# A diffusion block on one core: the half chunk that two heads share in row and column tiles, and LN2's scale and shift of batch 0 on two engines

## Chip, core, metric

One core of a Trainium2 chip runs the whole block. The metric is device time in microseconds (us), median over executions.

## The reference, cut to what matters

```python
B, N, D = (2, 256, 1152); F = 4 * D; H = 2; Dh = D // H          # Dh = 576 = 4.5 * 128
mod = (_silu(c) @ w_mod).reshape(B, 6, 1, D)
shift_a, scale_a, gate_a, shift_m, scale_m, gate_m = [mod[:, i] for i in range(6)]
h = _layernorm(x, axis=-1) * (1 + scale_a) + shift_a
qkv = (h @ wqkv).reshape(B, N, 3, H, Dh)
attn = _softmax(jnp.einsum('bqhd,bkhd->bhqk', q, k) * Dh ** (-0.5), axis=-1)
a = jnp.einsum('bhqk,bkhd->bqhd', attn, v).reshape(B, N, D) @ wo
x = x + gate_a * a
h2 = _layernorm(x, axis=-1) * (1 + scale_m) + shift_m            # "LN2"
m = _gelu(h2 @ w_fc1) @ w_fc2                                    # "FC1", "FC2"
return x + gate_m * m
```

The features are worked on in nine chunks of 128. A head has 576 of them, so chunk 4 (`HC` in the code) holds the last 64 features of head 0 and the first 64 of head 1. That is the shared chunk.

## The kernel before, the parts that matter

The masks for the shared chunk are zero-padded copies of k and v, cleared by four memsets on GpSimd at the start:

```python
    kT4m = act.tile([P, H, T], BF16, name="kT4m")
    v4m = act.tile([P, NT, H, P], BF16, name="v4m")
    nc.gpsimd.memset(kT4m[HP:P, 0, :], 0.0)
    nc.gpsimd.memset(kT4m[0:HP, 1, :], 0.0)
    nc.gpsimd.memset(v4m[:, :, 0, HP:P], 0.0)
    nc.gpsimd.memset(v4m[:, :, 1, 0:HP], 0.0)
```

Evictions from PSUM alternate between VectorE and ScalarE by a counter (`evac`). A score tile is five matmuls of 128 rows, and one score tile goes ahead of each of the first eight V groups:

```python
        for i, cc in enumerate(chunks):              # score_tile(b, h, qt); five chunks a head
            if cc == HC:
                k_ap = kT4m[:, h, b * N:(b + 1) * N]
            else:
                k_ap = kT[:, cc, b * N:(b + 1) * N]
            nc.tensor.matmul(
                ps_s[:], qT[:, cc, q0:q0 + P], k_ap,
                start=(i == 0), stop=(i == len(chunks) - 1),
            )
        # ... [cut: maximum, Exp with row sum, scaling]
    for i, (pnl, t) in enumerate(v_order):
        fin = score_tile(*score_order[i]) if i < len(score_order) else None
        v_group(pnl, t)
```

In the values stage the shared chunk takes four matmuls a batch (two heads, two key tiles, `v4m` as the stationary operand), every other chunk two. Then come the Wo groups, with LN2's statistics, normalisation and a DMA transpose per row tile of 128 tokens (row tiles 0 and 1 are batch 0), and LN2's scale and shift of the transposed chunks, all of them on VectorE:

```python
    def ln2_modulate(b, k):
        h = hT[:, k, b * N:(b + 1) * N]
        return nc.vector.tensor_scalar(
            h, h, scale_m[:, k, b:b + 1], shift_m[:, k, b:b + 1], op0=ALU.mult, op1=ALU.add,
        )
    # ... [cut]
    BETWEEN = {2: (0, 1), 3: (5,)}      # chunks done inside the normalisation of row tiles 2 and 3
    # ... [cut]
    for o, (t, i) in enumerate(order):
        if o == len(order) - 1:
            ln2_modulate(0, 2)
            ln2_modulate(0, 3)
        wo_group(t, i, i < NPD - 1)
        if o:
            ln2_stats(*order[o - 1])
    ln2_modulate(0, 4)
    ln2_stats(*order[-1])
    for k in range(6, KD):
        ln2_modulate(0, k)
```

FC1 starts with batch 0, six output chunks side by side, chunk by chunk: six matmuls per LN2 chunk.

The end of the kernel: the product of the last FC2 group with the gate, the addition of x1, and a 32 KB transfer of the output. For all other output groups the addition is on GpSimd.

## Time and profile before

| | before |
|---|---|
| time, median of 3 | 248.32 us (248.09 to 248.48) |
| span of the profiled execution | 246.4 us |
| TensorE (PE) busy | 238.0 us, 97% |
| VectorE, ScalarE, GpSimd busy | 67.0, 62.5, 28.0 us |
| first score to first value matmul (starts) | 52.27 to 76.83 us |
| FC1 to FC2, first matmuls | 98.74 to 172.49 us |

The share of busy time says only that TensorE bounds the kernel. Where it loses time is read from the chain of waits, which is followed back from the last instruction. Its columns are start, duration (us), and engine, tile and line of the kernel.

```profile
76.99 4.37 PE pa L545 x40
81.36 4.40 PE pacc L588 x27
85.76 0.02 issue
85.78 0.57 DVE tmp L593
...
104.61 0.27 DVE hT L559
104.87 0.04 issue
104.92 20.03 PE pacc L637 x181
...
172.66 70.30 PE pacc L691 x468
```

From 85.8 to 104.9 us VectorE (DVE) leads the chain, since it makes LN2 for FC1 (`L637`). The timeline of TensorE alone shows what that costs: start, duration, line, tiles, shape, number, and in brackets the idle time before and what ended it.

```profile
98.26 0.65 PE L588 MATMUL pacc<-w_o,big 128*128 128x384 bf16 x3
98.74 1.47 PE L637 MATMUL pacc<-hT,w_f 128*128 128x256 bf16 x12
100.66 1.47 PE L637 MATMUL pacc<-hT,w_f 128*128 128x256 bf16 x12 [0.44 <-DVE hT L559]
102.69 1.75 PE L637 MATMUL pacc<-hT,w_f 128*128 128x256 bf16 x12 [0.56 <-DVE hT L559]
104.92 3.33 PE L637 MATMUL pacc<-hT,w_f 128*128 128x256 bf16 x29 [0.48 <-DVE hT L559]
```

Thirty-six matmuls at 0.109 us each would take 3.9 us; the 37th starts 6.2 us after the first. The bracketed waits sum to only 1.5 us, because the ends of matmuls are modelled: measure such a hole from start to start.

The scores, in the same view. Four whole chunks and the masked one follow each other at the common pace of 0.109 us, and the V group starts one such step after them:

```profile
54.27 0.60 PE L468 MATMUL ps_s<-big 128*128 128x256 bf16 x4
54.71 0.27 PE L468 MATMUL ps_s<-kT4m,big 128*128 128x256 bf16 x1
54.82 1.63 PE L492 MATMUL pacc<-w_v,hT 128*128 128x384 bf16 x9
```

And the last 4 us. The first line counts all packets; the second gives a queue's packets, megabytes and share of time; the last two are transfers with their size and the time from issue to landing.

```profile
DMA packets 288, 0.10 MB, mean 25 GB/s; under 512 B 160, under 2 KB 288, under 8 KB 288
q1 hardware_dynamic: 288, 0.10, 9.3%
...
out_dram<-o_sb SPq DMA_DIRECT2D x1, 64.0 KB, 1.5
out_dram<-o_sb SPq DMA_DIRECT2D x1, 32.0 KB, 1.5
```

### The profile page before, as it was taken

How to read it: one execution, taken by the hardware profiler on the slowest of the kernel's cores; microseconds unless marked ns; L12 is line 12 of the kernel's file. 1: busy time of each engine (PE TensorE's matmuls, PEld its weight loads, DVE VectorE, ACT ScalarE, POOL GpSimd, SP SyncE). 2: the span in 40 equal slices, each digit the busy share in tenths (PEclk: the TensorE clock that was granted, in tenths of full speed). 3: DMA queues.
4: the chain of work that ended last, by engine and by line, in shares of the span. 5: the costliest groups of instructions: out<-in, count | busy, mean ns of one | idle time of the engine just before them, and what ended most of it. 6: DMA issues, size and time to landing. Idle time of an engine off the chain costs nothing.

```text
span 246.4 us, 3980 instructions
## 1 busy us (share of the span) xinstructions
PE 238.0 (97%) x1700; PEld 143.9 (58%) x1711; DVE 67.0 (27%) x184; ACT 62.5 (25%) x124; POOL 28.0 (11%) x43
## 2 busy tenths in 40 slices
PE   6999999999999999799999999999999999999994
PEld 2585444456657666588854444444666666666674
DVE  2852461335444598940000000000011000000001
ACT  6631341243423322361432233222000000000000
POOL 4000000031000234100000003100011212111111
PEclk9999999999999999999999999999999999999999
DMA  6999999999996998239999999990000000000100
GB/s 225 326 335 362 368 331 388 391 390 395 282 376 157 401 392 112 48 66 395 392 391 345 327 292 269 326 343 26 0 16 19 16 17 16 19 17 16 34 17 16
DMA packets 47373, 53.29 MB, mean 216 GB/s; under 512 B 8427, under 2 KB 34171, under 8 KB 47355
## 3 DMA queue, kind: packets, MB, share of 16 engines
q1 hardware_dynamic: 39840, 50.14, 60.9%
q10 hardware_dynamic: 6939, 1.71, 4.8%
q0 software_dynamic: 576, 1.19, 1.4%
q8 instruction: 13, 0.21, 0.4%
q14 instruction: 5, 0.04, 0.1%
HBM read 50.14 MB, written 1.19 MB: 208 GB/s over the span
## 4 chain that ended last, share of the span: by engine, by line
PE 88%; DVE 7%; DMA 2%; ACT 1%; issue 1%; DVEq 0%; ACTq 0%
PE pacc L691 29%; PE pacc L637 27%; PE pacc L492 7%; PE pacc L440 7%; PE pk L269 4%; PE pk L302 2%; PE pwarm L162 2%; PE pacc L588 2%; PE pa L545 2%; PE ps_s L468 2%; DVE stats L602 2%; PE pn L385 1%; DVE tmp L593 1%; DMA hT<-xn 1%; PE pg L418 1%; DMA c_sb<-in_c_dram 1%
## 5 line engine op out<-in xcount | busy, mean ns | idle before, releaser
L637 PE MATMUL pacc<-hT,w_f 128*128 128x256 bf16 (+1 forms) x427 | 70.9, 325 | 1.9 <-DVE hT L559 1.5
L691 PE MATMUL pacc<-w_f,gT 128*128 128x384 bf16 (+2 forms) x468 | 70.5, 314 | 0.0
L637 PEld LDWEIGHTS <-w_f 128*128 128x128 bf16 x432 | 42.1, 98 | 30.1 <-issue 2.5
L691 PEld LDWEIGHTS <-gT 128*128 128x128 bf16 x468 | 44.4, 98 | 26.2
L697 DVE TENSOR_TENSOR tmp<-pacc,gate 128x384 f32<-128x384 f32 (+2 forms) x13 | 6.8, 527 | 88.2 <-PE pacc L691 88.2
L669 ACT ACTIVATE gT<-pacc 128x512 bf16<-128x512 f32 x24 | 14.3, 597 | 32.2 <-PE pacc L637 32.2
L699 POOL TENSOR_TENSOR o_sb<-tmp,x 128x384 bf16<-128x384 f32 (+1 forms) x12 | 11.7, 971 | 73.8 <-DVE tmp L697 73.8
L492 PE MATMUL pacc<-w_v,hT 128*128 128x384 bf16 x108 | 19.2, 326 | 0.0
L440 PE MATMUL pacc<-hT,w_q 128*128 128x512 bf16 x79 | 17.7, 379 | 0.1
L588 PE MATMUL pacc<-w_o,big 128*128 128x384 bf16 x108 | 17.7, 326 | 0.0
L429 POOL DMA_DIRECT2D gates_dram<-nat x8 | 4.3, 543 | 93.5 <-DVE nat L426 93.5
L588 PEld LDWEIGHTS <-big 128*128 128x128 bf16 x108 | 10.6, 98 | 6.9
L492 PEld LDWEIGHTS <-hT 128*128 128x128 bf16 x108 | 10.4, 98 | 6.3 <-issue 0.5
L269 PE MATMUL pk<-big,w_k 128*128 128x256 bf16 (+2 forms) x88 | 13.3, 292 | 0.5 <-ACT big L256 0.4
L440 PEld LDWEIGHTS <-w_q 128*128 128x128 bf16 x81 | 7.8, 98 | 9.7 <-DMA w_q<-in_wqkv_dram 0.3
L426 DVE CAST nat<-pg 2x288 bf16<-2x288 f32 x4 | 1.8, 450 | 37.0 <-PE pg L418 36.9
L594 POOL TENSOR_TENSOR x<-tmp,x_sb 128x384 f32<-128x384 f32 x8 | 7.3, 914 | 35.9 <-DVE tmp L593 35.9
L269 PEld LDWEIGHTS <-w_k 128*128 128x128 bf16 x90 | 7.5, 97 | 3.4 <-DMA w_k<-in_wqkv_dram 0.3
L658 ACT ACTIVATE gT<-pacc 128x512 bf16<-128x512 f32 x12 | 6.6, 596 | 10.8 <-PE pacc L637 10.8
L162 PE MATMUL pwarm<-zeros 128*128 128x512 bf16 x18 | 7.3, 571 | 1.2 <-DVE eps_t L93 1.2
L593 DVE TENSOR_TENSOR tmp<-pacc,gate 128x384 f32<-128x384 f32 x12 | 6.6, 547 | 2.4 <-PE pacc L588 2.4
L288 DVE TENSOR_SCALAR big<-pacc 128x512 bf16<-128x512 f32 x5 | 3.5, 692 | 13.7 <-PE pacc L440 13.7
(94 smaller groups left out, 154.2 us busy)
## 6 DMA issues: line engine op xcount, KB each, us to landing
w_f<-in_w_fc_dram SPq DMA_DIRECT2D x14, 864.0 KB, 8.9
w_f<-in_w_fc_dram SPq DMA_DIRECT2D x2, 2592.0 KB, 12.4
w_f<-in_w_fc_dram SPq DMA_DIRECT2D x2, 1728.0 KB, 10.2
w_shift_a<-in_w_mod_dram SPq DMA_DIRECT2D x3, 864.0 KB, 11.5
w_q<-in_wqkv_dram SPq DMA_DIRECT2D x3, 864.0 KB, 12.1
w_gate_a<-in_w_mod_dram SPq DMA_DIRECT2D x3, 864.0 KB, 10.1
w_v<-in_wqkv_dram SPq DMA_DIRECT2D x3, 864.0 KB, 13.4
w_shift_m<-in_w_mod_dram SPq DMA_DIRECT2D x3, 864.0 KB, 15.3
```

The costliest lines, as they stand in the source:

```text
L162: nc.tensor.matmul(dst[:], zeros[:, 0:P], zeros[:], start=True, stop=True)
L269: nc.tensor.matmul(pk[m][:, c0:c1], w_k[:, k, m * P:(m + 1) * P], hT0[:, k, c0:c1], start=(k == 0 and c0 == 0), stop=(k == KD - 1), skip_g ...
L440: nc.tensor.matmul(pacc[:], w_q[:, k, m * P:(m + 1) * P], hT[:, k, :], start=(k == 0), stop=(k == KD - 1),)
L492: nc.tensor.matmul(pacc[:], hT[:, k, t * P:(t + 1) * P], w_v[:, k, pnl * PW:(pnl + 1) * PW], start=(k == 0), stop=(k == KD - 1),)
L588: nc.tensor.matmul(pacc[:], aT[:, k, t * P:(t + 1) * P], w_o[:, k, c0:c1], start=(k == 0), stop=(k == KD - 1),)
L593: nc.vector.tensor_tensor(tmp[:], pacc[:], gate_a[:, b, c0:c1], op=ALU.mult)
L594: (nc.gpsimd if pool_add else nc.vector).tensor_tensor(x1[:, t, c0:c1], tmp[:], x_sb[:, t, c0:c1], op=ALU.add)
L637: nc.tensor.matmul(dst, w_f1[m // KD][:, k, ml * P:(ml + 1) * P], hT[:, k, c0:c1], start=start, stop=(k == KD - 1), **kw,)
L669: nc.scalar.activation(gT[:, m, :], pacc[:], ACT.Gelu_apprx_tanh)
L691: nc.tensor.matmul(pacc[:], gT[:, kk, t * P:(t + 1) * P], w_f2[j][:, r, c0 - n * PW:c0 - n * PW + cw], start=(kk == 0), stop=(kk == KF - 1),)
L697: nc.vector.tensor_tensor(tmp[:], pacc[:], gate_m[:, b, c0:c0 + cw], op=ALU.mult)
L699: (nc.vector if last else nc.gpsimd).tensor_tensor(o_sb[:], tmp[:], x1[:, t, c0:c0 + cw], op=ALU.add)
```

## The change

The intent has two parts. First, the zero padding wastes half of each shared-chunk matmul; with 64 rows (scores) or 64 columns (values) each, the two heads' halves can run in two parts of the array at once. Second, LN2's scale and shift of batch 0 no longer all queue on VectorE: ScalarE takes chunks 2, 3, 5 and 7.

```diff
-    kT4m = act.tile([P, H, T], BF16, name="kT4m")
-    v4m = act.tile([P, NT, H, P], BF16, name="v4m")
-    nc.gpsimd.memset(...)                        # [cut: four of them]
     def k_evac(m):
-        if m == HC:
-            evac(kT4m[0:HP, 0, :], pk[m][0:HP, :])
-            evac(kT4m[HP:P, 1, :], pk[m][HP:P, :])
-        else:
-            evac(kT[:, m, :], pk[m][:])
+        evac(kT[:, m, :], pk[m][:])
+    def half(h):
+        return slice(h * HP, (h + 1) * HP)
+    def score_pair(b, qt):                       # replaces score_tile(b, h, qt)
+        ps = [acc_tile([P, N], "ps_s") for _ in range(H)]
+        for h in range(H):
+            whole = range(0, HC) if h == 0 else range(HC + 1, KD)
+            for cc in whole:
+                nc.tensor.matmul(ps[h][:], qT[:, cc, q0:q0 + P], kT[:, cc, b * N:(b + 1) * N],
+                                 start=(cc == whole[0]), stop=False)
+        for h in range(H):
+            nc.tensor.matmul(ps[h][:], qT[half(h), HC, q0:q0 + P], kT[half(h), HC, b * N:(b + 1) * N],
+                             start=False, stop=True)
         # ... [cut: maximum, Exp, scaling, now for two tiles]
-        c4 = HC * P - pnl * PW                   # [cut: the copies into v4m]
+    SCORES_AT = {0: (0, 0), 1: (0, 1), 3: (1, 0), 4: (1, 1)}
+    TRANSPOSES_AT = {3: 0, 7: 1}
         # ... [cut: the old order of the scores, and the loop that uses these two]
                     if cc == HC:                 # values, inside the loop over key tiles
+                        for h in range(H):
+                            nc.tensor.matmul(dst[half(h), :, :], vt[:, half(h)], attnT(b, h, kc),
+                                             start=(kc == 0), stop=(kc == TPB - 1))
         # ... [cut: the whole chunks, as before; the lines that this replaces]
-    def ln2_modulate(b, k):
+    def ln2_modulate(b, k, eng="d"):
+        if eng == "a":
+            return nc.scalar.activation(h, h, ACT.Identity, bias=shift_m[:, k, b:b + 1],
+                                        scale=scale_m[:, k, b:b + 1])
-    BETWEEN = {2: (0, 1), 3: (5,)}
+    BETWEEN = {2: ((0, "d"), (1, "d"), (2, "a"), (3, "a")), 3: ((8, "d"),)}
-        if o == len(order) - 1:
-            ln2_modulate(0, 2)
-            ln2_modulate(0, 3)
+        last = o == len(order) - 1
+        if last:
+            ln2_modulate(0, 4)
         wo_group(t, i, i < NPD - 1)
         if o:
             ln2_stats(*order[o - 1])
-    ln2_modulate(0, 4)
+        if last:
+            ln2_modulate(0, 5, "a")
+            ln2_modulate(0, 7, "a")
+            ln2_modulate(0, 6)
     ln2_stats(*order[-1])
-    for k in range(6, KD):
-        ln2_modulate(0, k)
```

More of the change, by code (lines that the diff above doesn't have):

```diff
@@ L144 @@
     HP = Dh - HC * P
-    kT4m = act.tile([P, H, T], BF16, name="kT4m")
-    v4m = act.tile([P, NT, H, P], BF16, name="v4m")
-    nc.gpsimd.memset(kT4m[HP:P, 0, :], 0.0)
-    nc.gpsimd.memset(kT4m[0:HP, 1, :], 0.0)
-    nc.gpsimd.memset(v4m[:, :, 0, HP:P], 0.0)
-    nc.gpsimd.memset(v4m[:, :, 1, 0:HP], 0.0)
     early = small.tile([P, 2], FP32, name="early", tag="early", bufs=1)
@@ L446 @@
             gate_a = gate_natural(0, w_gate_a)
-    def head_chunks(h):
-        return list(range(HC + 1)) if h == 0 else list(range(HC, KD))
+    def half(h):
+        return slice(h * HP, (h + 1) * HP)
     n_s = B * H * TPB
@@ L456 @@
     attnT_all = soft[:, 3 * n_s * N:4 * n_s * N].rearrange("p (i n) -> p i n", n=2 * N)
-    attn_tiles = {}
-    def score_tile(b, h, qt):
-        chunks = head_chunks(h)
+    def score_pair(b, qt):
         q0 = b * N + qt * P
-        ps_s = acc_tile([P, N], "ps_s")
-        for i, cc in enumerate(chunks):
-            if cc == HC:
-                k_ap = kT4m[:, h, b * N:(b + 1) * N]
-            else:
-                k_ap = kT[:, cc, b * N:(b + 1) * N]
+        ps = [acc_tile([P, N], "ps_s") for _ in range(H)]
+        for h in range(H):
+            whole = range(0, HC) if h == 0 else range(HC + 1, KD)
+            for cc in whole:
+                nc.tensor.matmul(
+                    ps[h][:], qT[:, cc, q0:q0 + P], kT[:, cc, b * N:(b + 1) * N],
+                    start=(cc == whole[0]), stop=False,
+                )
+        for h in range(H):
@@ L468, in score_tile @@
             nc.tensor.matmul(
-                ps_s[:], qT[:, cc, q0:q0 + P], k_ap,
-                start=(i == 0), stop=(i == len(chunks) - 1),
-            )
-        negmax = small.tile([P, 1], FP32, name="negmax", tag="negmax")
-        nc.vector.reduce_max(negmax[:], ps_s[:], axis=AX.X, negate=True)
-        si = (b * H + h) * TPB + qt
-        e_sb = e_all[:, si, :]
-        rowsum = small.tile([P, 1], FP32, name="rowsum", tag="rowsum")
-        nc.scalar.activation(e_sb, ps_s[:], ACT.Exp, bias=negmax[:], scale=1.0, accum_out=rowsum[:])
@@ L478, in score_tile @@
-        attn = attn_all[:, si, :]
-        attn_tiles[(b, h, qt)] = attn
+                ps[h][:], qT[half(h), HC, q0:q0 + P], kT[half(h), HC, b * N:(b + 1) * N],
+                start=False, stop=True,
+            )
+        parts = []
+        for h in range(H):
+            negmax = small.tile([P, 1], FP32, name="negmax", tag="negmax")
+            nc.vector.reduce_max(negmax[:], ps[h][:], axis=AX.X, negate=True)
+            si = (b * H + h) * TPB + qt
+            rowsum = small.tile([P, 1], FP32, name="rowsum", tag="rowsum")
+            nc.scalar.activation(
+                e_all[:, si, :], ps[h][:], ACT.Exp, bias=negmax[:], scale=1.0, accum_out=rowsum[:]
+            )
+            parts.append((si, rowsum))
@@ L481, in finish @@
         def finish():
-            rs = small.tile([P, 1], FP32, name="rs", tag="rs")
-            nc.vector.reciprocal(rs[:], rowsum[:])
-            nc.vector.tensor_scalar_mul(attn, e_sb, rs[:])
+            for si, rowsum in parts:
+                rs = small.tile([P, 1], FP32, name="rs", tag="rs")
+                nc.vector.reciprocal(rs[:], rowsum[:])
+                nc.vector.tensor_scalar_mul(attn_all[:, si, :], e_all[:, si, :], rs[:])
         return finish
@@ L496, in v_group @@
         evac(v_sb[:, t, pnl * PW:(pnl + 1) * PW], pacc[:])
-        c4 = HC * P - pnl * PW
-        if 0 <= c4 and c4 + P <= PW:
-            evac(v4m[:, t, 0, 0:HP], pacc[:, c4:c4 + HP])
-            evac(v4m[:, t, 1, HP:P], pacc[:, c4 + HP:c4 + P])
     def attn_transpose(i):
@@ L505, in attn_transpose @@
         nc.scalar.dma_start_transpose(attnT_all[:, i, :].rearrange("p (c n) -> p c n", n=P), pair)
-    score_order = [(b, h, qt) for b in range(B) for h in range(H) for qt in range(TPB)]
+    SCORES_AT = {0: (0, 0), 1: (0, 1), 3: (1, 0), 4: (1, 1)}
+    TRANSPOSES_AT = {3: 0, 7: 1}
     v_order = [(pnl, t) for pnl in range(NPD) for t in range(NT)]
@@ L510 @@
     for i, (pnl, t) in enumerate(v_order):
-        fin = score_tile(*score_order[i]) if i < len(score_order) else None
+        fin = score_pair(*SCORES_AT[i]) if i in SCORES_AT else None
         v_group(pnl, t)
@@ L514 @@
             fin()
-        if i >= 2 and i % 2 == 0 and i // 2 <= B * H:
-            attn_transpose(i // 2 - 1)
+        if i in TRANSPOSES_AT:
+            for h in range(H):
+                attn_transpose(TRANSPOSES_AT[i] * H + h)
         if i == 8:
@@ L536 @@
             for ci, cc in enumerate(cp):
-                if cc == HC:
-                    srcs = [(v4m[:, b * TPB + kc, h, :], attnT(b, h, kc))
-                            for h in range(H) for kc in range(TPB)]
-                else:
-                    h = 0 if cc < HC else 1
-                    srcs = [(v_sb[:, b * TPB + kc, cc * P:(cc + 1) * P], attnT(b, h, kc))
-                            for kc in range(TPB)]
-                for i, (lhsT, rhs) in enumerate(srcs):
-                    av = nc.tensor.matmul(
-                        pa[:, ci, :].rearrange("p (q n) -> p q n", n=P), lhsT, rhs, start=(i == 0), stop=(i == len(srcs) - 1),
-                    )
+                dst = pa[:, ci, :].rearrange("p (q n) -> p q n", n=P)
+                for kc in range(TPB):
+                    vt = v_sb[:, b * TPB + kc, cc * P:(cc + 1) * P]
+                    if cc == HC:
+                        for h in range(H):
+                            nc.tensor.matmul(
+                                dst[half(h), :, :], vt[:, half(h)], attnT(b, h, kc),
+                                start=(kc == 0), stop=(kc == TPB - 1),
+                            )
+                    else:
+                        av = nc.tensor.matmul(
+                            dst, vt, attnT(b, cc // (HC + 1), kc),
+                            start=(kc == 0), stop=(kc == TPB - 1),
+                        )
             if b == 0 and cp == cpairs[0]:
@@ L554 @@
     mv2 = small.tile([P, NT, 2], FP32, name="mv2", tag="mv2", bufs=1)
-    def ln2_modulate(b, k):
+    def ln2_modulate(b, k, eng="d"):
         h = hT[:, k, b * N:(b + 1) * N]
+        if eng == "a":
+            return nc.scalar.activation(
+                h, h, ACT.Identity, bias=shift_m[:, k, b:b + 1], scale=scale_m[:, k, b:b + 1],
+            )
         return nc.vector.tensor_scalar(
@@ L565, in ln2_normalize @@
         nc.scalar.activation(rstd[:], mv2[:, t, 1:2], ACT.Sqrt, bias=eps_t[:], scale=1.0)
-        for k in between:
-            ln2_modulate(0, k)
+        for k, eng in between:
+            ln2_modulate(0, k, eng)
         nc.vector.reciprocal(rstd[:], rstd[:])
@@ L614 @@
             ln2_stats(*order[o - 1])
-    ln2_modulate(0, 4)
+        if last:
+            ln2_modulate(0, 5, "a")
+            ln2_modulate(0, 7, "a")
+            ln2_modulate(0, 6)
     ln2_stats(*order[-1])
-    for k in range(6, KD):
-        ln2_modulate(0, k)
     w_f2 = []
```

## The prediction

> **What bounds the kernel now.** TensorE: busy 238.0 of 246.4 us (first part of the page), clock 1.000, 88% of the chain of waits. From 30 us to the end of the values stage the chain stays on TensorE. The hole that matters is where LN2 meets FC1: the chain goes to VectorE at 85.8 us and returns to TensorE at 104.9. In the timeline Wo's matmuls end and FC1 starts at 98.74 us; its first 36 matmuls (LN2 chunks 0 to 5, six each, 109 ns apart) need 3.9 us, but the 37th starts at 104.92. So 2.2 us of stall: after chunks 1, 3 and 5 FC1 waits for the scale-and-shift of hT (0.44, 0.56, 0.48 us, plus weight-load gaps), because VectorE is saturated (busy 4.66 of 5 us from 95 to 100).
>
> **What the change does, costed.**
>
> 1. LN2 of batch 0. VectorE keeps chunks 0,1,4,6,8 (0.28 to 0.35 us each), ScalarE, idle there, takes 2,3,5,7 (the same form elsewhere: 0.495 us mean). Walking the queues: 0,1 by 98.7 as before; 2,3 on ScalarE by about 99.2 (needed 100.1); 4 by 100.2 (needed 101.4); ScalarE then normalises the next row tile (1.35 us) and issues its transpose, which holds its queue 1.3 us, so 5 lands at about 102.3 (needed 102.1: stall 0.25 us); 6, 7, 8 in time. FC1's chunk 8 ends at about 105.0 instead of 106.9: **-1.9 us**, all on the critical path, since FC1 and FC2 hardly stall after it.
>
> 2. Scores. 40 matmuls become 32 whole ones and 8 half-row ones in 4 concurrent pairs. At 0.11 us a matmul (five take 0.55 us in the chain) the ideal saving is 4 x 0.11 = 0.44 us. But every pair enters and leaves a tiling mode. The Trainium skill, "TensorEngine Tiling (Array Packing)", Key Properties, says a change of mode drains TensorE. The trace agrees for column tiles: from the last v matmul to the first of the modulation 0.26 us start to start instead of 0.162, and out again 0.1 more: 0.2 us a round trip. If row mode costs the same, each pair costs 0.2 + 0.11 against 0.22: **+0.35 us** in all.
>
> 3. Values. Shared chunk: four matmuls (0.44 us) a batch become two concurrent pairs. The trace shows column tiles overlapping well (36 matmuls of 288 columns start within 1.00 us). 0.22 + 0.2 against 0.44: **about 0**.
>
> 4. Removed: masked copies, eight 64-column evictions (0.2 us each), memsets on GpSimd; none is on the chain: 0. The eviction parity flips, so the last q panel leaves on ScalarE just before the Exp table load (1.28 us) and the first Exp starts 0.8 us later; six accumulators absorb it: 0. Transposes are issued in twos, still early enough: 0.
>
> **Sum.** 248.3 - 1.9 + 0.35 = **246.7 us**, 8 in 10 within **245.8 to 247.7**. Chances: faster by over 2%: 0.02; within 2%: 0.97; slower: 0.01.
>
> **What would show it.** (1) FC1 waits for hT below 0.6 us in total; its first to its 54th matmul in 6.2 us instead of 8.1. (2) From the first score to the first value matmul 0.2 to 0.5 us more; gaps of 0.1 us on both sides of each half pair, whose two start almost together. (3) Value stage still 4.4 us. (4) No new wait of TensorE for accumulators or qT.
>
> **What would make it wrong.** Row mode may switch more cheaply than column mode (up to 0.8 us better), or half weights may not be prefetched across it (worse). ScalarE's transpose issue may hold chunks 5 and 7 longer, giving back up to 1 us. The late Exp table could delay accumulators in the first V groups.

## The result, and the profile after

| | before | after |
|---|---|---|
| median | 248.34 us | 247.86 us (247.35 to 248.36, 4 runs) |
| ratio | | 0.9982 (0.9959 to 1.0004) |
| first score to first value matmul | 24.56 us | 25.08 us |
| first value to first Wo matmul | 4.36 us | 4.38 us |
| first FC1 to first FC2 matmul | 73.75 us | 72.03 us |
| end of the last VectorE operation to the last landing | 1.49 us | 2.15 us |

A ratio is the mean time of one kernel's runs over that of the other's runs of the same rounds, so not quite the ratio of the medians that are quoted. Executions over 1.5% slower than the fastest of the same kernel are left out of the means. The stage lengths are differences of start times in the two profiled executions.

The kernel gained 0.5 us where 1.6 were forecast. The interval of this ratio still includes no gain at all; that of again_after, 0.9960 to 0.9985, does not. The chain of waits after shows LN2's part working, and one wait left: chunk 5 on ScalarE (ACT) sits behind the issue of a transpose (`ACTq`).

```profile
77.24 0.87 PE pa L541 x8
...
100.78 0.02 issue
100.80 1.31 ACTq L580
102.11 0.05 issue
102.16 0.61 ACT hT L557
102.77 0.04 issue
102.81 41.83 PE pacc L639 x285
...
171.20 70.30 PE pacc L693 x468
```

TensorE's own timeline, to set against the five lines before the change:

```profile
98.20 0.98 PE L589 MATMUL pacc<-w_o,big 128*128 128x384 bf16 x5
99.01 3.44 PE L639 MATMUL pacc<-hT,w_f 128*128 128x256 bf16 x30
102.81 5.40 PE L639 MATMUL pacc<-hT,w_f 128*128 128x256 bf16 x48 [0.36 <-ACT hT L557]
```

Thirty matmuls (chunks 0 to 4) need 30 x 0.109 = 3.3 us, and the 31st starts 3.8 us after the first. So 0.5 us of stall is left of 2.2, which is the 1.72 us that the FC1 stage shows.

The scores after. The half pair (`64*128`) stands between whole matmuls:

```profile
54.76 1.04 PE L456 MATMUL ps_s<-big 128*128 128x256 bf16 x8
55.73 0.28 PE L461 MATMUL ps_s<-big 64*128 64x256 bf16 x2
55.94 0.50 PE L488 MATMUL pacc<-w_v,hT 128*128 128x384 bf16 x2
```

The two halves of the first pair start 3 ns apart (53.068 and 53.071 us). But the eight whole matmuls begin at 54.76 and the V group at 55.94: 1.18 us for a pair, where two score tiles took 2 x 0.55 = 1.10. The weight loads (PEld) of the whole chunks start 0.16 us before their matmuls (54.60 and 54.76). At the row tiles they no longer run ahead: the loads of the halves and of the V group start with their matmuls (55.72 and 55.73, 55.94 and 55.94):

```profile
54.60 0.92 PEld L456 LDWEIGHTS <-big 128*128 128x128 bf16 x8
55.72 0.10 PEld L461 LDWEIGHTS <-big 64*128 64x128 bf16 x2 [0.21 <-issue]
55.94 0.28 PEld L488 LDWEIGHTS <-hT 128*128 128x128 bf16 x3
```

And the last 4 us of the changed kernel:

```profile
q1 hardware_dynamic: 288, 0.10, 9.3%
q14 instruction: 1, 0.01, 1.0%
...
out_dram<-o_sb SPq DMA_DIRECT2D x1, 64.0 KB, 1.5
out_dram<-o_sb SPq DMA_DIRECT2D x1, 32.0 KB, 2.1
```

A packet of the instruction queue q14 (8 KB, at 242.96 us, 0.63 us long) falls beside the last output transfer, which lands after 2.1 us instead of 1.5. A transfer is reported done by sixteen semaphore updates; the Trainium skill, "Trainium Kernel Development and Optimization", Key Constraints, says that DMA semaphores increment by 16, and the trace agrees. Fifteen of the sixteen came by 243.70 us, the last at 244.37. Before the change the last q14 packet lay at 232.94 us, beside nothing urgent.

**Theory A.** The four gains and losses are -1.72 (LN2), +0.52 (scores), +0.02 (values) and +0.66 us (tail), together -0.5. The tail belongs to the change: the removed GpSimd memsets moved GpSimd's last instruction fetch. Two q14 packets of the two kernels do not settle that, but counting helps: in both traces, and in the ten that followed, the last q14 packet starts when GpSimd has exactly 68 recorded instructions behind it, while the other engines' counts differ (in these two, VectorE 202 and 203, SyncE 85 and 95). Four instructions fewer at the start mean that the 68th comes four instructions later, and at the end GpSimd has two records per output group and works at the pace of one full group in about 5.9 us.

One thing must not be added to this sum: the spans of the two profiled executions differ by 0.8 us (246.4 and 245.6), because the first score also starts 0.27 us earlier in the trace after (52.00 against 52.27). That is taken as scatter: again_after, the same kernel, starts it at 52.61, and the twelve traces lie between 52.00 and 52.72 without order.

**Rivals.** (B) The tail is chance. (C) LN2's split is worth less than the profiled execution shows. (D) The scores lose through their new order or a late q panel, not through the tiles.

### The profile page after: what moved, and what is told of

Same layout as the page of the kernel before. It is cut to its first block, busy times and chain, and to the rows that moved or that the text cites. A ratio compares the mean times of both kernels' runs of the same rounds, so it can differ in the third digit from the quotient of the medians.

```text
span 245.6 us, 3980 instructions
## 1 busy us (share of the span) xinstructions
PE 238.3 (97%) x1711; PEld 142.5 (58%) x1711; DVE 64.7 (26%) x175; ACT 63.3 (26%) x124; POOL 26.5 (11%) x39
## 4 chain that ended last, share of the span: by engine, by line
PE 86%; DVE 4%; DMA 4%; ACT 2%; issue 1%; ACTq 1%; SPq 0%; DVEq 0%
PE pacc L693 29%; PE pacc L639 27%; PE pacc L488 7%; PE pacc L430 7%; PE pk L263 4%; DMA w_scale_a<-in_w_mod_dram 3%; PE pk L292 2%; PE pacc L589 2%; PE pa L541 2%; PE pn L375 1%; PE ps_s L456 1%; DMA hT<-xn 1%; DVE stats L603 1%; DVE tmp L594 1%; PE pg L408 1%; ACT xn L579 1%
## 5 line engine op out<-in xcount | busy, mean ns | idle before, releaser
L488 PE MATMUL pacc<-w_v,hT 128*128 128x384 bf16 x108 | 18.6, 327 | 0.0
L250 ACT ACTIVATE big<-pt,scale_a 128x256 bf16<-128x256 bf16 (+1 forms) x12 | 4.6, 434 | 9.2 <-PE pt L241 7.4
```

The costliest lines, as they stand in the source:

```text
L488: nc.tensor.matmul(pacc[:], hT[:, k, t * P:(t + 1) * P], w_v[:, k, pnl * PW:(pnl + 1) * PW], start=(k == 0), stop=(k == KD - 1),)
```

## The experiments

All gave correct results. Every ratio is to the kernel before. Where an experiment is set against a kernel of another call, the lengths of the stages and the ratios decide, not the times. "Family" in one expectation means the kernels that are compared with pool4.

### again_after: the changed kernel once more

No edit. 

> The changed kernel once more, for its spread and a second trace. Theory A (instruction fetch): its GpSimd instruction block is fetched again at about 243 us, beside the last output transfer, whose landing takes 2 us or more instead of 1.5; ratio to before 0.997 to 0.999. Theory B (chance): in this trace the fetch lies elsewhere or the last output lands in 1.5 us all the same.

Measured: 247.74 us (247.54 to 247.91), ratio 0.9973 (0.9960 to 0.9985). The q14 packet is there again, at 243.59 us, with 68 GpSimd records before it; the last output lands after 1.9 us (a little under the expected 2), its sixteenth part 0.41 us behind the fifteenth. The stages repeat: 25.07 us for scores and V, 72.04 us for FC1. So B is in doubt: the collision is no accident of one execution, though its size varies.

### pool4: four memsets that nobody needs

```diff
+    kT4m = act.tile([P, H, T], BF16, name="kT4m")
+    v4m = act.tile([P, NT, H, P], BF16, name="v4m")
+    nc.gpsimd.memset(...)                        # the four of before; the tiles are not read
```

> The changed kernel with the four GpSimd memsets that it removed put back, on tiles that nobody reads. Theory A: the GpSimd fetch moves back to about 231 to 233 us, the last output lands in 1.5 us, and the kernel is 0.6 to 0.7 us faster than the changed one (about 247.2 us, ratio 0.995). Theory B, that the tail is chance, or that four memsets cost something themselves: no difference from the changed kernel (0.998), or slower.

Measured: 247.05 us (247.03 to 247.21), ratio 0.9947 (0.9934 to 0.9959), so 0.7 us faster than the changed kernel (247.74). The last q14 packet is at 232.03 us, and the last 4 us are clean again:

```profile
DMA packets 288, 0.10 MB, mean 25 GB/s; under 512 B 160, under 2 KB 288, under 8 KB 288
q1 hardware_dynamic: 288, 0.10, 9.3%
...
out_dram<-o_sb SPq DMA_DIRECT2D x1, 32.0 KB, 1.5
```

Four dead instructions made the kernel faster. The executions also lie closer together: a range of 0.18 us against 0.37. B falls.

### before_pool_minus4: the same, the other way round

```diff
-    nc.gpsimd.memset(...)
+    nc.vector.memset(...)                        # all four, in the kernel before
```

> The kernel before with its four memsets on VectorE instead of GpSimd; nothing else. Theory A: the last GpSimd fetch moves from 233 us to about 244 us and the 16th part of the last output lands 0.4 to 0.7 us late, so the kernel is 0.4 to 0.7 us slower (ratio 1.002 to 1.003). Rival: the position of the fetch does not matter, ratio 1.000.

Measured: 248.9 us (248.5 to 250.25), ratio 1.003 (1.0012 to 1.0048); without the one execution of 250.25 us, at a clock of 0.990, the means give 1.002, still as expected. The lengths of the stages stay as before (24.56, 4.37 and 73.77 us), so the memsets on VectorE cost nothing there. The fetch moved to 244.53 us, again after the 68th GpSimd record, and the last output again lands about 0.7 us later:

```profile
q1 hardware_dynamic: 288, 0.10, 9.3%
q14 instruction: 1, 0.01, 1.0%
...
out_dram<-o_sb SPq DMA_DIRECT2D x1, 32.0 KB, 2.1
```

The kernel before, untouched but for the engine of four memsets, loses what the changed kernel lost. The tail is settled as a consequence of GpSimd's instruction count.

How the fetch delays the transfer can be read from the packets themselves, which the kept traces list. The last transfer has 144 packets, 128 of 256 B and 16 of 4 B. In the trace after, 135 of them have started by 243.34 us; the other nine, one sixteenth (eight of 256 B and one of 4 B), start only from 243.581 us on, and the fetch packet ends at 243.584. It is the same in all four traces whose fetch falls beside the last transfer: the nine start 3 or 4 ns before the fetch ends. The longer the fetch takes, the later they land: for fetches of 0.46, 0.59, 0.63 and 0.63 us, the sixteenth part comes 0.41, 0.56, 0.67 and 0.67 us after the fifteenth. In the eight other traces it comes 0.01 or 0.02 us after it. So one sixteenth of the transfer waits for the fetch. That the two share one DMA engine is the plain reading, but no record names the engine of a packet, so that last step is argued, not shown.

### ln2_only: the LN2 split in the kernel before

The edit is the LN2 part of the change, all else as before; GpSimd's instructions stay. 

> The kernel before with the LN2 split alone. If the two traces tell the truth (FC1 start to FC2 start 73.9 to 72.2 us) and the tail stays where it was: 246.6 us, ratio 0.993. If the profiled execution of the changed kernel was a lucky one and the split is worth less on the chip: 247.3 or more, ratio 0.996 or above.

Measured: 246.64 us (246.5 to 247.0), ratio 0.9932 (0.9919 to 0.9946); FC1 stage 72.06 us, last q14 packet at 231.32 us. C falls. This half of the change alone does better than the whole.

### tiles_only: everything but the LN2 split

The edit is the change without its LN2 part. 

> The changed kernel with LN2 as before: row and column tiles and the removed memsets alone. Theory A: first score to first value matmul +0.5 us, values 0, tail +0.66: about 249.4 us, ratio 1.0045. As the prediction costed it, without the tail: 248.7, ratio 1.0015.

Measured: 249.43 us (249.28 to 249.73), ratio 1.0042 (1.0029 to 1.0055); scores and V 25.08 us, q14 packet at 245.29 us, last landing 2.0 us after issue. The tiles with their removed memsets are a loss of 1 us.

### pair_masked: the order of the change without row tiles

```diff
-                ps[h][:], qT[half(h), HC, q0:q0 + P], kT[half(h), HC, b * N:(b + 1) * N],
+                ps[h][:], qT[:, HC, q0:q0 + P], kT4m[:, h, b * N:(b + 1) * N],
```

The base is pool4. The two masked halves of k are written by one copy on each engine, with the eviction counter advanced once, so that all later evictions keep their engines. 

> The changed kernel with the four memsets back (pool4, the reference of this call's family), its score halves as whole 128-row matmuls against zero-padded k, in the same order. Theory switch: the round trip into row tiles costs more than the concurrency gives, so this is about 0.37 us faster than pool4 (246.7 against 247.05), and first score to first value matmul falls from 25.07 to about 24.7 us. Rival order: the 0.5 us come from the new order and the late last q panel; then it stays at 25.07.

Measured: 246.61 us (246.46 to 246.98), ratio 0.9930 (0.9917 to 0.9943), against 247.05 for pool4 (0.9947, 0.9934 to 0.9959). It was run at another time. These two intervals overlap a little, so the stage decides. First score to first value matmul: 24.66 us, where pool4 has 25.07. The pair in the timeline:

```profile
55.37 1.04 PE L468 MATMUL ps_s<-big 128*128 128x256 bf16 x8
56.24 0.38 PE L473 MATMUL ps_s<-kT4m,big 128*128 128x256 bf16 x2
56.46 0.33 PE L500 MATMUL pacc<-w_v,hT 128*128 128x384 bf16 x1
```

From 55.37 to 56.46 is 1.09 us. Twice the arithmetic in the shared chunk, and 0.09 us less per pair. Of the 0.51 us, row tiles cost 0.41 and the order 0.10 (24.66 against 24.56 before). D explains only a fifth.

### quad: half as many changes of mode

```diff
-    def score_pair(b, qt):
+    def score_quad(b):          # 16 whole matmuls of both query tiles, then the four halves
-    SCORES_AT = {0: (0, 0), 1: (0, 1), 3: (1, 0), 4: (1, 1)}
+    SCORES_AT = {0: 0, 3: 1}
```

The base is pool4. 

> pool4 with the scores of a batch issued together: 16 whole matmuls, then four halves in one stretch of row tiles: two round trips instead of four. Theory switch (0.2 us a round trip, halves truly concurrent): 25.07 falls to about 24.67 us, kernel 0.4 us faster than pool4. Rival: halves run one after the other and the switch is cheap; then no difference.

Measured: 246.56 us (246.5 to 246.78), ratio 0.9931 (0.9919 to 0.9943); first score to first value matmul 24.65 us, 0.42 less than pool4. Row tiles are used just as much, but entered twice instead of four times.

```profile
52.29 2.01 PE L463 MATMUL ps_s<-big 128*128 128x256 bf16 x16
54.23 0.39 PE L470 MATMUL ps_s<-big 64*128 64x256 bf16 x4
54.56 1.64 PE L498 MATMUL pacc<-w_v,hT 128*128 128x384 bf16 x9
```

The starts around the halves are 54.026 (whole), 54.231, 54.235, 54.351, 54.355 (halves) and 54.556 (V). Two halves start 4 ns apart, and the next two 0.12 us after them: the concurrency is real. But each border takes 0.20 us from start to start where a matmul of this width takes 0.109. That is 0.1 us in and 0.1 us out, 0.2 a round trip. What happens inside a border was not tested. The weight load that no longer runs ahead takes about 0.1 us (98 ns for a whole chunk), as long as a border costs, so whether the time goes to the array's drain, to the load behind it, or to both stays open.

### q8_vector: the last q panel on VectorE, a miss

```diff
+        if m == KD - 1:
+            evac_i += 1
+            nc.vector.tensor_scalar_mul(qT[:, m, :], pacc[:], attn_scale)
```

The base is pool4. 

> pool4 with the last q panel evicted on VectorE as before, not on ScalarE. If the first score pair loses time to that eviction (gap of 0.20 us at the weight load in the changed kernel's trace), first score to first value falls by 0.1 to 0.2 us; kernel 0.1 to 0.2 us faster than pool4, at the edge of what the timing resolves. If not, no difference.

Measured: 247.3 us (247.07 to 247.32), ratio 0.9957 (0.9945 to 0.9968): not faster than pool4; first score to first value matmul 25.17 us, 0.1 more. The engine was not the point. A pair reaches the last q panel after seven matmuls, whichever engine evicts it; ScalarE's eviction takes 0.60 us and VectorE's 0.69, so VectorE made the wait longer. What causes the wait is the order of the pair.

### ln2_chunk5: the wait that was left in FC1

```diff
-    BETWEEN = {2: ((0, "d"), (1, "d"), (2, "a"), (3, "a")), 3: ((8, "d"),)}
+    BETWEEN = {2: ((0, "d"), (1, "d"), (2, "a"), (3, "a"), (5, "a")), 3: ((8, "d"),)}
-            ln2_modulate(0, 5, "a")
```

The base is ln2_only. 

> ln2_only with LN2 chunk 5 ahead of ScalarE's normalisation and transpose issue. If the one wait left in FC1 (0.36 us, chunk 5 behind the transpose issue) is what separates the trace from -2.1 us: FC1 start to FC2 start falls from 72.05 to about 71.7 us, kernel 246.3 us (ratio 0.9918). If chunk 7 or the later row-tile transpose then binds instead: no gain.

Measured: 246.0 us (245.78 to 246.19), ratio 0.9902 (0.9888 to 0.9917); FC1 stage 71.51 us, 0.55 less than ln2_only. FC1 runs without a break from its first matmul on:

```profile
98.86 9.33 PE L641 MATMUL pacc<-hT,w_f 128*128 128x256 bf16 x84
```

The gain is 0.55 and not the 0.36 of the bracket, again because the bracket counts from a modelled end.

### grouped: tiles entered as seldom as the order allows

```diff
-        for qt in range(TPB):
-            q0 = b * N + qt * P
-            for h in range(H):
+        for h in range(H):
+            for qt in range(TPB):
+                q0 = b * N + qt * P
-    cpairs = [(0, 1), (2, 3), (4, 5), (6, 7), (8,)]
+    cpairs = [(0, 1), (2, 3), (5, 6), (7, 8)]
-        for cp in cpairs:
+        for cp in (cpairs + [(HC,)] if b == 0 else [(HC,)] + cpairs):
```

The base is quad, and chunk 5 is early as in ln2_chunk5. 

> Best guess: four memsets kept, scores of a batch in one stretch of row tiles with head 0 of both query tiles first (so the last q panel is not waited for), shared value chunks of both batches in one stretch of column tiles, chunk 5 early. Theory switch: first score to first value 24.65 to about 24.5 us, values 4.38 to about 4.18 us, FC1 -0.36: about 245.9 to 246.0 us (ratio 0.9905). Rival, tiles never pay here: not below ln2_chunk5 (246.3).

Measured: 245.82 us (245.77 to 246.37), ratio 0.9903 (0.9886 to 0.9919). In the trace the values stage fell as expected (4.16 us against 4.38), and first score to first value matmul is 24.55 us, what it was without tiles (24.56). This profiled execution also waited 0.6 us for the load of the q weights, before the scores, which the edit does not touch. The timing does not separate it from ln2_chunk5 (0.9902). So even grouped, the tiles add nothing here that the timing resolves, though the trace shows 0.2 us less in the values stage; the simplest of the fastest versions is ln2_chunk5. Both beat both kernels, by about 1% against before.

## Why the prediction was wrong, point by point

The forecast was 246.7 us (245.8 to 247.7); measured were 247.86 and 247.74. The class, within 2%, was right.

| term | predicted | measured | by |
|---|---|---|---|
| LN2 split | -1.9 | -1.7 | FC1 stage; ln2_only |
| scores | +0.35 | +0.51 | 0.41 tiles, 0.10 order: pair_masked |
| values | about 0 | +0.02 | values stage |
| removed memsets, copies and evictions | 0 | +0.7 | pool4, before_pool_minus4 |
| sum | -1.6 | -0.5 | |

1. **The step that failed** is the fourth: "Removed: masked copies, eight 64-column evictions (0.2 us each), memsets on GpSimd; none is on the chain: 0." It is true that none was on the chain, and still their removal moved the time. Without the four memsets, GpSimd's last instruction fetch came 10 us later, beside the last output transfer, which lies at the very end of the program: +0.7 us. The prediction had named four ways to be wrong, and this was none of them.
2. **LN2: mechanism right, size slightly off.** Chunk 5 was the only late one, as the walk of the queues said, and for the reason it gave; the stall is 0.5 us start to start instead of 0.25. The 54th FC1 matmul comes 6.3 us after the first (53 x 0.109 + 0.5), where 6.2 was forecast. Part of this is in the trace: ScalarE takes 0.59 us for the chunk, where the prediction took 0.495 from another line, and FC1 needs the chunk 3.3 us after its start (30 x 0.109) instead of the 3.4 that were forecast (102.1 less 98.74); the transpose issue took the 1.3 us that were forecast.
3. **Scores: mechanism right, size off.** The Trainium skill, "TensorEngine Tiling (Array Packing)", Key Properties, says that a change of tiling mode drains TensorE. The round trip of 0.2 us, read from column tiles in the trace before, held for row tiles as well (quad: -0.42 us for two trips fewer). The runs show what a border costs; that it is the drain which takes this time, they do not show. What was left out is 0.1 us for the order: the prediction saw no new wait for qT ("No new wait of TensorE for accumulators or qT"), and there was one, before chunk 8 of the first pair.
4. **Concurrency** came as the skill says: "TensorE: Matmul & The Clock Gate", Part 3, gives a start difference of about 4 ns for tiles in different row groups, and the traces show 3 and 4 ns. It saves one 0.11 us matmul per pair, half of what entering and leaving costs.
5. **Values** came out even, as forecast, for the same reason: 0.2 us saved, 0.2 paid a batch.

Left open: why GpSimd fetches after its 68th record and why one fetch packet takes longer than another (0.63 and 0.46 us in the two traces of the changed kernel, which gives the delays of 0.67 and 0.41), which DMA engine carried the fetch, and what a border of a tiling mode spends its 0.1 us on.

## What to carry to other kernels

Count the borders of a tiling mode, not the tiles: here a round trip cost 0.2 us, two 256-column matmuls' worth, and a concurrent pair saves 0.11. So one pair in a stretch lost 0.1 us, two broke even (scores of grouped, 24.55 against 24.56), and four gained 0.2 (values of grouped, 4.16 against 4.38). Look at the last microseconds of a trace before removing "free" instructions: an instruction fetch that slides beside the last transfer can delay its landing (here by 0.4 to 0.7 us, and the kernel's end with it), and a kernel can be tuned around it by a few dead instructions on the engine concerned (as long as nothing else is edited afterwards). When parts of a change pull in opposite directions, time them apart: here one half alone was 1 us better than the whole.

## What the Trainium skill lacked or had wrong

- "TensorEngine Tiling (Array Packing)", Key Properties and Theoretical Speedup: the drain is named without a size. Here it was 0.1 us in and 0.1 us out, for 64-row tiles and for 64- and 32-column tiles, so that an "up to 2x" on one pair of 256-column matmuls turned into a loss of 0.1 us.
- Instruction fetches: "Runtime: NRT & Kernel Launch", Instruction fetch mechanics, says that a sequencer fetches its instructions over a DMA queue of its own and that the cost is mostly hidden. That such a fetch can hold up a data transfer, and for how long, was found on no page; it belongs to "DMA: Bandwidth & Descriptors", Queues, rings and completion order. The traces show 13 packets of 16 KB on q8 and 5 of 8 KB on q14 during a run, and a last output transfer of 32 KB that lands 0.4 to 0.7 us later when one of them falls beside it.
